# A fused attention and gated MLP kernel: k3 loaded and crossed over ahead of q2 and v2, a gate moved, two bursts regrouped

## The chip, the cores and the metric

The kernel runs on one core of a Trainium2 chip. The metric is the device time of one execution in microseconds (us). Before the change the median of three runs is 245.85 us (245.5 to 246.13).

## The reference

Eight batches of eight heads, 576 tokens and 64 dimensions per head. A packed query p of 32 rows per head first attends to k and v, then q attends to what comes out; the result, as 4608 rows of 512, goes through an MLP whose gate is h * cos(h):

```python
def sm_attn(qq, kk, vv):
    s = scale * np.matmul(qq, kk.transpose(0, 1, 3, 2))
    a = np.exp(s - np.max(s, axis=-1, keepdims=True))
    a = a / (np.sum(a, axis=-1, keepdims=True) + 1e-09)
    return np.matmul(a, vv)
p_packed = sm_attn(p, k, v)                  # (8, 8, 32, 64)
out = sm_attn(q, p_packed, p_packed)         # (8, 8, 576, 64)
x = out.transpose(0, 2, 1, 3).reshape(4608, 512)
h = x @ w_in                                 # 512 -> 2048
return (h * np.cos(h)) @ w_out               # 2048 -> 512
```

## The kernel before

The work goes batch by batch, b = 0 to 7. For a batch, `s1` (L148) makes the scores of p against k, with their exponential on ACT; `a1_pe` or `a1_xbar` (L169, L164) transposes them, on PE or with a DMA transpose; `pp` (L179) multiplies them with v, and `pp_T` (L194) transposes what comes out. `ppw` (L201) multiplies that with w_in in four groups of 512 columns, so that the second attention and the first MLP product become one product with PPW. `s2` (L227) makes the scores of q, `sums2` and `normalise` (L234, L244) their softmax, a2n. Then `h_mm` (L256) makes h in 16 pieces of 128 columns (fc 0 to 15): four matmuls on PE, a cosine on ACT (L267), a product on DVE (L270). The last product, with w_out, is written as a generator, `out_gen` (L343); each step is one matmul of 512 columns, and at the end of a chunk come a copy from PSUM to `osb` and output DMAs on SP's queue. `fill(n)` (L368) takes n such steps of an earlier batch, to occupy PE between other things.

The order on each engine is written out by hand. A front (the code between two slots) holds the attention of the next batch, with `fill` calls in its gaps. `slot(s, hooks, keep, heavy, last)` (L492) holds the 16 `h_mm` of batch s, spreads the remaining output steps over them by weight, leaves `keep` steps over for the next front, and calls hooks, each behind a given fc. A pair in `heavy` gives extra weight to the outputs at an fc, and how many of them come behind the hook. Slots 3 to 6 have one hook, `tiled` (L513), at fc 7: PPW groups 2 and 3 and pp of the next batch in one place, with one evacuation on ACT and one on DVE; pp uses an unused corner of a PSUM bank of `h_mm` (`spare`). Slot 2 has PPW groups 2 and 3 at fc 6 (`pw2`, L509) and pp(3) at fc 9, copied by ACT.

Batches 0 and 1 have their k and q transposed on PE (`pe_T`, L107). In slot 1, k2 is transposed on PE too (`tk2`, L523, at fc 8 and the last third at fc 10), while q2 and k3 are crossed over: `xbar` (L100) issues a DMA transpose from SP's queue. From then on q and k are always crossed over, and a1 from batch 3 on (`a1_xbar`).

Loads are issued by POOL (`load`, L92), in order. `behind(t)` (L96) makes POOL copy one element of a crossed tensor, so that the loads after it wait until that crossing has landed; below this is called the gate. PSUM has three double banks for most of this (`psa`), two single ones for outputs (`O`). There are two buffers each for loaded k and v, one for loaded q, two for crossed k, one for crossed q, and four for `osb`.

Of the kernel before, what the change touches and what calls it, by code (L numbers as in the profile page):

```python
# [15 lines left out]
def kernel(  # L16
# [46 lines left out]
    V, ACT, G = nc.vector, nc.scalar, nc.gpsimd  # L63
# [16 lines left out]
    bf, xT, a1T, sums1, r1, rs1 = {}, {}, {}, {}, {}, {}  # L80
    a2u, lns, a2n, PPW = {}, {}, {}, {}

    def copy(eng, out, in_):
        if eng is ACT:
            ACT.copy(out=out, in_=in_)  # L85
        else:
            eng.tensor_copy(out=out, in_=in_)  # L87

    def psa(dt=FP32):
        return psum["A"].tile([128, 2, 512 if dt == FP32 else 1024], dt, name="psA", tag="A")  # L90

    def load(n, b):  # L92
        bf[n, b] = bf_pool.tile([TP, H, C * D], BF16, name=n + "bf", tag=n + "bf", bufs=1 if n == "q" else 2)
        G.dma_start(out=bf[n, b], in_=srcs[n][b].rearrange("h (p c) d -> p h (c d)", c=C))

    def behind(t):  # L96

        G.tensor_copy(out=gate, in_=t)  # L98

    def xbar(n, b):  # L100
        t = xT[n, b] = att_pool.tile([128, H * 3, TP], BF16, name=n + "T", tag=n + "T", bufs=2 if n == "k" else 1)
        nc.sync.dma_start_transpose(out=t, in_=bf[n, b].rearrange("p h x -> p (h x)"))

    def one(dt=FP32):
        return psum["H"].tile([128, 512 if dt == FP32 else 1024], dt, name="psH", tag="H")

    def pe_T(n, b, engs=(V, V, V), groups=(0, 1, 2), own=None):  # L107
        if 0 in groups:
            xT[n, b] = att_pool.tile([128, H * 3, TP], BF16, name=n + "T", tag=n + "T", bufs=2 if n == "k" else 1)
        t = xT[n, b]  # L110
        flat = bf[n, b].rearrange("p h x -> p (h x)")
        for i in groups:
            ps = own(BF16) if own else psa(BF16)[:, 0, :]
            for j in range(8):
                o = 8 * i + j
                nc.tensor.transpose(ps[:, j * TP:(j + 1) * TP], flat[:, o * 128:(o + 1) * 128],  # L116
                                    ident[0:TP, 0:TP])
            to = t[:, 8 * i:8 * i + 8].rearrange("p a x -> p (a x)"), ps[:, 0:8 * TP]
            if engs[i] is None:
                return to  # L120
            copy(engs[i], *to)

    def bank(dt=FP32):
        return O.tile([128, 512 if dt == FP32 else 1024], dt, name="ot", tag="ot")

    def pack_p(b0, b1, flat=None):
        ng = 2 * (b1 - b0)
        if flat is None:
            flat = psa(BF16).rearrange("p a x -> p (a x)")
        for g in range(ng):  # L130
            nc.tensor.transpose(flat[:, g * 128:(g + 1) * 128],
                                p_bf[:, 2 * b0 + g].rearrange("p t d -> p (t d)"), ident)
        V.tensor_copy(out=P2[:, b0:b1].rearrange("p b h n -> p (b h n)"), in_=flat[:, 0:ng * 128])
# [45 lines left out]
    def pp(b, eng=V, own=None):  # L179

        ps = own() if own else psa()[:, 0, :]
        for y in range(2):
            for j in range(C):
                c = 2 * (j % 3) + j // 3
                for x in range(4):
                    nc.tensor.matmul(ps[32 * x:32 * x + 32, y * D:(y + 1) * D],  # L186
                                     a1T[b][0:TP, y, j, 32 * x:32 * x + 32],
                                     bf["v", b][:, 2 * x + y, c * D:(c + 1) * D],
                                     start=(j == 0), stop=(j == C - 1))
        t = pp_sb[b % 2].rearrange("p a d -> p (a d)")  # L190
        copy(eng, t[:, 0:2 * D], ps[:, 0:2 * D])
        copy(eng, t[:, 2 * D:3 * D], ps[:, 0:D])

    def pp_T(b, eng=V, own=None):  # L194
        ps = own(BF16) if own else psa(BF16)[:, 0, :]
        t = pp_sb[b % 2].rearrange("p a d -> p (a d)")
        for i in range(2):
            nc.tensor.transpose(ps[:, i * 128:(i + 1) * 128], t[:, i * D:i * D + 128], ident)
        copy(eng, ppT[b % 2].rearrange("p i x n -> p (i x n)"), ps[:, 0:256])
# [34 lines left out]
    def sums2(b, y):  # L234
        if b not in lns:
            lns[b] = att_pool.tile([128, 2, S], FP32, name="lns", tag="lns")
        ps = psa()
        for e in range(2):
            nc.tensor.matmul(ps[:, e, 0:HS], ones_blk, a2u[b][:, y, e * HS:(e + 1) * HS],  # L239
                             start=True, stop=True)  # L240
        ACT.activation(out=lns[b][:, y].rearrange("p (e x) -> p e x", e=2),  # L241
                       in_=ps[:, :, 0:HS], func=AF.Ln)
# [55 lines left out]
    def h_rest(b):  # L298

        t = psa()  # L300
        for fc in range(NFC):
            for y in range(2):
                nc.tensor.matmul(t[:, fc // 8, (fc % 8) * 64:(fc % 8) * 64 + 64],  # L303
                                 PPW[b][:, y, fc * 128:(fc + 1) * 128], a2n[b][:, y, 512:576],
                                 start=(y == 0), stop=(y == 1))
        cs = cos_pool.tile([128, 2, 512], BF16, name="cosR", bufs=1)
        ACT.activation(out=cs, in_=t, func=AF.Sin, bias=PI_HALF)
        j0 = (b % 2) * 64
        V.tensor_tensor(out=joint[b // 2][:, :, j0:j0 + 64],
                        in0=t.rearrange("p a (f x) -> p (a f) x", x=64),  # L310
                        in1=cs.rearrange("p a (f x) -> p (a f) x", x=64), op=ALU.mult)
# [53 lines left out]
    def to_do():  # L365
        return sum(n for _, n in filler)

    def fill(n):  # L368
        while n > 0 and filler:
            next(filler[0][0])  # L370
            filler[0][1] -= 1
            if filler[0][1] == 0:
                filler.pop(0)
            n -= 1
# [9 lines left out]
    def dup_p(a, b, eng):  # L384
        for t in range(2):
            eng.tensor_copy(out=p_bf[:, a:b, t, :], in_=p_raw[:, a:b, :])

    def warm(n, wps=None, w=None):
        wps, w = bank() if wps is None else wps, wz if w is None else w
        for _ in range(n):  # L390
            nc.tensor.matmul(wps, w[:, 0:128], w, start=True, stop=True)  # L391
# [45 lines left out]
    pack_p(1, 2, bank(BF16))  # L437
    warm(1)
    sums2(0, 0)
    pe_T("k", 1, (V, V, V), (0,), own=bank)  # L440
    sums2(0, 1)
    pe_T("k", 1, (V, V, V), (1,), own=bank)
    pe_T("k", 1, (V, V, V), (2,), own=bank)
    warm(1)
    normalise(0)
    s1(1)
# [23 lines left out]
    pe_T("q", 1, (ACT, V, V), (1, 2), own=one)  # L470
    rest15()
    warm(3, one())
    load("v", 2)
    load("q", 2)
    load("k", 3)
    dup_p(4, 2 * B, G)
    banks(3)
    set_filler(0)
    s2(1)
    ppw(1, 0, V)  # L480
    fill(2)
    sums2(1, 0)
    fill(1)
    sums2(1, 1)
# [7 lines left out]
    def slot(s, hooks, keep=0, heavy={}, last=None):  # L492


        left = to_do() - keep
        weight = [1 + heavy.get(fc, (0, 0))[0] for fc in range(NFC)]
        for fc in range(NFC):
            rest = h_mm(s, fc)
            if fc == NFC - 1 and last:
                last()  # L500
            rest()
            quota = (left * sum(weight[:fc + 1])) // sum(weight) - (left + keep - to_do())
            behind = min(quota, heavy[fc][1]) if fc in heavy else quota
            fill(quota - behind)
            while hooks and hooks[0][0] == fc:
                hooks.pop(0)[1]()
            fill(behind)

    def pw2(b, n, eng=None):  # L509
        ppw(b, n, eng)  # L510
        ppw(b, n + 1, eng)

    def tiled(b):  # L513


        own, later = spare[0], []
        for n in (2, 3):
            later += ppw(b, n, (ACT, V)[n - 2], later=True)
        later[0]()
        pp(b + 1, V, own=lambda: own)  # L520
        later[1]()
# [10 lines left out]
    def cross(n, b):  # L532
        return lambda: xbar(n, b)

    osb_eng[0] = ACT
    slot(1, [(2, lambda: pw2(1, 2, (ACT, V))), (4, lambda: h_rest(0)), (6, lambda: pack_p(2, 4)), (8, tk2),
             (9, cross("q", 2)), (10, lambda: pe_T("k", 2, (V, V, ACT), (2,))), (12, cross("k", 3))], 4, {2: (1, 2), 4: (3, 5)})
    ACT.preload_act_table_set(EXP_SET)
    osb_eng[0] = V
    behind(xT["k", 3][0:1, 0, 0:1])  # L540
    load("v", 3)
    load("q", 3)
    load("k", 4)
# [33 lines left out]
        load(n, b)  # L577
    fill(9)
    osb_eng[0] = ACT
    slot(2, [(6, lambda: pw2(2, 2)), (9, lambda: pp(3, ACT))], 10, {6: (3, 3), 9: (1, 1)}, lambda: pp_T(3, V))  # L580

    for s in range(3, B):
        nxt = s + 1 < B
# [67 lines left out]
```

## Time and profile before

| | us |
|---|---|
| median of three runs | 245.85 |
| profiled execution, in all | 246.25 |
| its span | 244.5 |
| PE busy in the span | 231.6 |
| ACT, DVE, POOL busy | 166.8, 162.2, 38.1 |
| s2(1) to the first h matmul of slot 1 | 35.63 to 40.60 |
| slot 1: first to last h matmul | 40.60 to 61.25 |
| first gate, second gate (POOL) | 67.16, 89.59 |
| slot 2, first h matmul | 75.09 |
| slot 3, first h matmul | 100.61 |

PE is TensorE's matmuls, PEld its weight loads, DVE VectorE, ACT ScalarE, POOL GpSimd, SP the sync engine; SPq and POOLq are their DMA queues. L12 is line 12 of the kernel. In a line of the timeline come the start, the duration, the engine, the line, the operation, output and inputs, and the count; in brackets stands how long the engine was idle before it and what ended that. A busy time counts overlapping instructions once. In a line of the DMA view the last number is the time from issue to landing. In a line of a table by stretch come the stretch, its length, and for each engine its busy time with the number of instructions; then the granted clock of PE as a share of full speed, the DMA share and GB/s.

### The profile page before, as it was taken

How to read it: one execution, taken by the hardware profiler on the slowest of the kernel's cores; microseconds unless marked ns; L12 is line 12 of the kernel's file. 1: busy time of each engine (PE TensorE's matmuls, PEld its weight loads, DVE VectorE, ACT ScalarE, POOL GpSimd, SP SyncE). 2: the span in 40 equal slices, each digit the busy share in tenths (PEclk: the TensorE clock that was granted, in tenths of full speed). 3: DMA queues.
4: the chain of work that ended last, by engine and by line, in shares of the span. 5: the costliest groups of instructions: out<-in, count | busy, mean ns of one | idle time of the engine just before them, and what ended most of it. 6: DMA issues, size and time to landing. Idle time of an engine off the chain costs nothing.

```text
span 244.5 us, 5460 instructions
## 1 busy us (share of the span) xinstructions
PE 231.6 (95%) x2220; PEld 128.6 (53%) x2255; DVE 162.2 (66%) x257; ACT 166.8 (68%) x269; POOL 38.1 (16%) x61
## 2 busy tenths in 40 slices
PE   7979899999999999999999999999999999999994
PEld 3444254566446464556456554656455645665453
DVE  3349987776568876678758775878657878774001
ACT  2349999778568787877787687858797676774110
POOL 8532330210130023000500510030101010011000
PEclk9999999999999999999999999999999999999999
DMA  6999999999789999999999899989192111312133
GB/s 90 202 211 206 204 208 227 194 232 169 161 137 168 209 174 169 218 185 201 154 214 217 160 213 223 201 163 186 53 198 50 39 46 43 84 29 61 44 86 86
DMA packets 64152, 37.37 MB, mean 153 GB/s; under 512 B 36624, under 2 KB 59536, under 8 KB 64128
## 3 DMA queue, kind: packets, MB, share of 16 engines
q0 software_dynamic: 23184, 18.81, 50.8%
q1 hardware_dynamic: 40704, 18.09, 36.1%
q8 instruction: 17, 0.28, 0.4%
q10 hardware_dynamic: 240, 0.13, 0.2%
q14 instruction: 7, 0.06, 0.1%
HBM read 37.22 MB, written 9.44 MB: 191 GB/s over the span
## 4 chain that ended last, share of the span: by engine, by line
PE 76%; DVE 6%; DMA 5%; issue 2%; ACT 1%; ACTq 0%
PE ot L351 45%; PE psA L263 21%; DMA a1T<-a 5%; DVE gT L295 3%; PE psA L213 3%; PE psA L143 2%; PE ot L337 1%; PE psA L239 1%; DVE PPW L87 1%; PE psA L186 1%; ACT cosT L294 0%; PE psA L116 0%; DVE qT L87 0%; PE psA L303 0%; DVE a1T L87 0%
## 5 line engine op out<-in xcount | busy, mean ns | idle before, releaser
L351 PE MATMUL ot<-w_out_bf,gT 128*128 128x512 bf16 x485 | 128.9, 379 | 1.8 <-issue 1.3
L270 DVE TENSOR_TENSOR gT<-psA,cosT 128x576 bf16<-128x576 f32 x112 | 83.4, 757 | 22.3 <-ACT cosT L267 21.2
L267 ACT ACTIVATE cosT<-psA 128x576 bf16<-128x576 f32 x112 | 73.0, 653 | 24.8 <-PE psA L263 23.5
L263 PE MATMUL psA<-a2n,PPW 128*128 128x288 bf16 x448 | 73.4, 286 | 0.6 <-issue 0.2
L351 PEld LDWEIGHTS <-gT 128*128 128x128 bf16 x512 | 48.2, 98 | 39.7 <-issue 4.6
L263 PEld LDWEIGHTS <-PPW 128*128 128x128 bf16 x448 | 43.7, 98 | 30.5 <-DVE PPW L87 0.5
L87 DVE CAST PPW<-psA 128x1024 bf16<-128x1024 f32 (+1 forms) x24 | 26.8, 1131 | 6.8 <-PE psA L213 6.6
L85 ACT COPY osb<-ot 128x512 f32<-128x512 f32 (+1 forms) x23 | 13.1, 569 | 16.4 <-PE ot L351 14.1
L87 DVE COPY osb<-ot 128x512 f32<-128x512 f32 (+2 forms) x15 | 9.7, 645 | 20.4 <-PE ot L337 17.2
L274 POOL COPY joint<-gT 128x512 bf16<-128x512 bf16 x14 | 8.5, 618 | 76.7 <-DVE gT L270 76.7
L249 DVE SCALAR_TENSOR_TENSOR a2n<-a2u,r,lns 128x576 bf16<-128x576 bf16 x16 | 12.4, 814 | 9.2 <-ACT lns L247 9.2
L241 ACT ACTIVATE lns<-psA 128x576 f32<-128x576 f32 x16 | 10.4, 651 | 8.2 <-PE psA L239 7.7
L152 ACT ACTIVATE a<-psA 128x576 bf16<-128x576 f32 x16 | 10.3, 647 | 8.3 <-PE psA L143 8.2
L98 POOL COPY gate<-kT 1x1 bf16<-1x1 bf16 x5 | 0.9, 180 | 77.3 <-DMA kT<-kbf 77.3
L351 PE MATMUL ot<-w_out_bf,joint 128*128 128x512 bf16 x45 | 11.5, 379 | 0.3 <-issue 0.2
L231 ACT ACTIVATE a2u<-psA,rs 128x576 bf16<-128x576 f32 x16 | 11.0, 737 | 1.1 <-PE psA L143 1.0
L247 ACT ACTIVATE lns<-lns 128x576 f32<-128x576 f32 x16 | 10.0, 673 | 0.0
L213 PE MATMUL psA<-w_in_bf,ppT 64*32 64x512 bf16 x224 | 9.8, 379 | 0.1
L391 PE MATMUL ot<-wz 128*128 128x512 bf16 (+1 forms) x15 | 7.9, 633 | 2.0 <-DVE wz L405 1.7
L295 DVE TENSOR_TENSOR gT<-psH,cosT 128x512 bf16<-128x512 f32 x15 | 9.3, 680 | 0.4 <-ACT cosT L294 0.4
L294 ACT ACTIVATE cosT<-psH 128x512 bf16<-128x512 f32 x15 | 8.4, 625 | 0.7 <-DVE gT L295 0.4
L289 PE MATMUL psH<-a2n,PPW 128*128 128x512 bf16 x28 | 7.3, 381 | 1.0 <-DVE PPW L87 0.8
(91 smaller groups left out, 171.6 us busy)
## 6 DMA issues: line engine op xcount, KB each, us to landing
kbf<-in_k_dram POOLq DMA_DIRECT2D x8, 576.0 KB, 14.3
vbf<-in_v_dram POOLq DMA_DIRECT2D x8, 576.0 KB, 8.5
qbf<-in_q_dram POOLq DMA_DIRECT2D x8, 576.0 KB, 11.0
out_dram<-osb SPq DMA_DIRECT2D x24, 192.0 KB, 2.7
out_dram<-osb SPq DMA_DIRECT2D x22, 128.0 KB, 2.4
w_in_bf<-in_moe_w_in_dram POOLq DMA_DIRECT2D x4, 512.0 KB, 16.3
w_out_bf<-in_moe_w_out_dram POOLq DMA_DIRECT2D x4, 512.0 KB, 20.9
out_dram<-osb SPq DMA_DIRECT2D x25, 64.0 KB, 2.1
```

The source lines that it names most:

```text
L85: ACT.copy(out=out, in_=in_)
L87: eng.tensor_copy(out=out, in_=in_)
L152: ACT.activation(out=a1[b % 2][:, y, :, 0:TP].rearrange("p (e m) x -> p e m x", e=2), in_=ps[y][:, :, 0:HS].rearrange("p e (m x) -> p e m ...
L213: nc.tensor.matmul(ps[y][32 * x:32 * x + 32, :], ppT[b % 2][r, 0, x, :], w_in_bf[r, x, n * 512:(n + 1) * 512], start=True, stop=True)
L231: ACT.activation(out=a2u[b][:, y].rearrange("p (e x) -> p e x", e=2), in_=ps[y][:, :, 0:HS], func=AF.Exp, scale=rs1[b][:, y:y + 1])
L241: ACT.activation(out=lns[b][:, y].rearrange("p (e x) -> p e x", e=2), in_=ps[:, :, 0:HS], func=AF.Ln)
L249: V.scalar_tensor_tensor(out=a2n[b][:, y], in0=a2u[b][:, y], scalar=r1[b][:, y:y + 1], in1=lns[b][:, y], op0=ALU.mult, op1=ALU.mult)
L263: nc.tensor.matmul(ps[:, e, 0:HS], PPW[b][:, y, fc * 128:(fc + 1) * 128], a2n[b][:, y, e * HS:(e + 1) * HS], start=(y == 0), stop=(y == 1))
L267: ACT.activation(out=csv, in_=ps[:, :, 0:HS], func=AF.Sin, bias=PI_HALF)
L270: V.tensor_tensor(out=gT[b][:, fc, :].rearrange("p (e x) -> p e x", e=2), in0=ps[:, :, 0:HS], in1=csv, op=ALU.mult)
L295: return lambda: V.tensor_tensor(out=gT[b][:, fc, 0:512], in0=ps, in1=cs, op=ALU.mult)
L351: nc.tensor.matmul(pss[c], w, w_out_bf[:, fc, :], start=(fc == 0), stop=(fc == NFC - 1))
```

## The change

Five edits. At the start, both `sums2` of batch 0 come ahead of the transposes of k1, which stay together. The three loads v2, q2, k3 are issued in the order k3, q2, v2. In the front ahead of slot 1, `fill(2)` becomes `fill(4)`. In slot 1, k3's crossing moves from fc 12 to fc 7, ahead of q2's (fc 9), and the gate waits for q2's crossing, not k3's. In slot 2, `tiled(2)` at fc 7 replaces `pw2` at fc 6 and `pp(3)` at fc 9.

```diff
     sums2(0, 0)
-    pe_T("k", 1, (V, V, V), (0,), own=bank)
     sums2(0, 1)
-    pe_T("k", 1, (V, V, V), (1,), own=bank)
-    pe_T("k", 1, (V, V, V), (2,), own=bank)
+    pe_T("k", 1, (V, V, V), own=bank)
...
+    load("k", 3)
+    load("q", 2)
     load("v", 2)
-    load("q", 2)
-    load("k", 3)
     dup_p(4, 2 * B, G)
...
     ppw(1, 0, V)
-    fill(2)
+    fill(4)
     sums2(1, 0)
...
     slot(1, [(2, lambda: pw2(1, 2, (ACT, V))), (4, lambda: h_rest(0)), (6, lambda: pack_p(2, 4)),
-             (8, tk2), (9, cross("q", 2)), (10, lambda: pe_T("k", 2, (V, V, ACT), (2,))), (12, cross("k", 3))],
+             (7, cross("k", 3)), (8, tk2), (9, cross("q", 2)), (10, lambda: pe_T("k", 2, (V, V, ACT), (2,)))],
             4, {2: (1, 2), 4: (3, 5)})
...
-    behind(xT["k", 3][0:1, 0, 0:1])
+    behind(xT["q", 2][0:1, 0, 0:1])
     load("v", 3)
     load("q", 3)
     load("k", 4)
...
-    slot(2, [(6, lambda: pw2(2, 2)), (9, lambda: pp(3, ACT))], 10, {6: (3, 3), 9: (1, 1)}, lambda: pp_T(3, V))
+    slot(2, [(7, lambda: tiled(2))], 10, {7: (5, 4)}, lambda: pp_T(3, V))
```

From slot 3 to the end, PE's list of instructions is the same in both kernels.

More of the change, by code (lines that the diff above doesn't have):

```diff
@@ L535 @@
     osb_eng[0] = ACT
-    slot(1, [(2, lambda: pw2(1, 2, (ACT, V))), (4, lambda: h_rest(0)), (6, lambda: pack_p(2, 4)), (8, tk2),
-             (9, cross("q", 2)), (10, lambda: pe_T("k", 2, (V, V, ACT), (2,))), (12, cross("k", 3))], 4, {2: (1, 2), 4: (3, 5)})
+    slot(1, [(2, lambda: pw2(1, 2, (ACT, V))), (4, lambda: h_rest(0)), (6, lambda: pack_p(2, 4)), (7, cross("k", 3)),
+             (8, tk2), (9, cross("q", 2)), (10, lambda: pe_T("k", 2, (V, V, ACT), (2,)))], 4, {2: (1, 2), 4: (3, 5)})
     ACT.preload_act_table_set(EXP_SET)
     osb_eng[0] = V
-    behind(xT["k", 3][0:1, 0, 0:1])
+    behind(xT["q", 2][0:1, 0, 0:1])
     load("v", 3)
```

## The prediction

> **What bounds the kernel now.** I read the busy times first, then the chain that ended last, then PE's busy time slot by slot, and last the queues of SP and POOL around the change.
>
> ```profile
> PE 231.6 (95%) x2220; PEld 128.6 (53%) x2255; DVE 162.2 (66%) x257; ACT 166.8 (68%) x269; POOL 38.1 (16%) x61
> ...
> PE 76%; DVE 6%; DMA 5%; issue 2%; ACT 1%; ACTq 0%
> ```
>
> The chain runs through PE. What can be won is PE's idle time, 244.5 - 231.6 = 12.9 us, and most of that lies outside the change: in the windows 0-36 us and from 232 us on, PE is idle 5.9 and 3.6 us. Next, PE in the five stretches from the first h matmul of slots 2, 3, 4, 5 and 6 to the transposes of pp that end the slot:
>
> ```profile
> core 0: us, PE busy (x) PEld busy (x) DVE busy (x) ACT busy (x) POOL busy (x), PEclk, DMA share, GB/s
> 75.09:90.70 15.61, 15.19 (x156) 9.39 (x157) 12.25 (x18) 12.35 (x21) 0.27 (x2) 1.00 1.24 180
> 100.61:117.13 16.52, 16.12 (x162) 10.10 (x163) 12.93 (x20) 12.08 (x20) 1.49 (x3) 1.00 1.19 195
> 126.97:143.67 16.70, 16.54 (x163) 10.25 (x165) 12.36 (x19) 12.36 (x21) 3.11 (x5) 1.00 1.08 192
> 153.48:170.18 16.70, 16.44 (x163) 10.25 (x165) 12.96 (x20) 11.98 (x20) 2.33 (x4) 1.00 1.05 189
> 179.99:196.70 16.71, 16.55 (x164) 10.26 (x166) 12.36 (x19) 12.37 (x21) 0.62 (x1) 1.00 0.32 72
> ```
>
> The second number is the stretch, the third PE's busy time. Slots 4 to 6, which have the merged burst (both late PPW groups and pp in one place), leave PE idle 0.16, 0.26 and 0.16 us, mean 0.19. Slot 2, which has the burst in two pieces, leaves 0.42. Slot 3 has the merged burst and yet leaves 0.40. The clock is granted in full everywhere.
>
> From PE's timeline, front 1 and slot 3's burst:
>
> ```profile
> 36.22 0.39 PE L351 MATMUL ot<-w_out_bf,gT 128*128 128x512 bf16 x1
> 37.11 0.41 PE L239 MATMUL psA<-a2u,ones_blk 128*128 128x288 bf16 x2 [0.51 <-ACT a2u L231]
> ...
> 109.11 0.55 PE L186 MATMUL psA<-vbf,a1T 96*32 96x64 bf16 x48 [0.19 <-DMA a1T<-a]
> ```
>
> In front 1, PE has run out of output matmuls (one of the two records is missing) and waits for the exponentials of s2(1). At 109.11, pp(4) waits for the crossing (the DMA transpose) of a1 of batch 4. Last, the DMA issues with their time to landing, each from a window at its issue: q2 and k3 at 35, and the crossing of a1 of batch 3 at 69.78:
>
> ```profile
> qbf<-in_q_dram POOLq DMA_DIRECT2D x1, 576.0 KB, 20.6
> kbf<-in_k_dram POOLq DMA_DIRECT2D x1, 576.0 KB, 22.8
> ...
> a1T<-a SPq DMA_TRANSPOSE x1, 14.4
> ```
>
> **Sums of batch 0 ahead of k1.** PE waits at 17.64 for k1's load; sums2(0,1) stands behind the first eight transposes of k1 and moves to about 16.95. Its logarithm on ACT comes at 17.4 instead of 18.44, so the two exponentials of normalise end near 19.2 instead of 20.24. But a2n on DVE (19.82) is queued behind the three copies of kT (18.19 to 19.90), and these wait for k1's load, which nobody moves. DVE then runs without a gap until 24. I take 0. The bounds: 0.2 us lost if the second and third copies came later, 0.15 won because ACT reaches the exponential of s1(1) sooner (20.29, while its matmuls begin at 19.70).
>
> **Two outputs sooner in front 1.** An output matmul costs 2.33 us / 10 = 0.217 us of PE (ten in a row, the last 0.38 long), not the 379 ns shown for one. Two records from 36.22 on fill PE until 36.65; sums2(1,0) starts at 37.11; two more end at 37.09. They fit into 0.46 us of waiting and leave slot 1, whose list has one output less ahead of h_rest and one less ahead of fc 11. Their inputs are there: step 9 of the outputs needs the second quarter of w_out, which lands 17.88 + 20.8 = 38.7; it comes at 38.44 + 3 x 0.217 = 39.1. Slot 1 must be PE-bound for the gain: PE is busy 21.16 of 21.50 us in 41-62.5. The tight places are pack_p (50.83, behind a DVE product that ends at 50.77, itself released by h_rest, which moves along) and fc 11, whose bank is free at 56.43 against 56.70. I take 0.40 of the 0.43; the lower bound is 0.
>
> **k3 ahead of q2 and v2, gate behind q2.** POOL issues k3 where v2 was (30.35), q2 unchanged (35.06), v2 where k3 was (35.83). They land in that order at the old times: 51.75, 35.06 + 20.6 = 55.66 and 35.83 + 22.8 = 58.63. v2 loses 6.9 us; pp(2) needs it only at 67.51. On SP, k3's crossing stands behind the four output DMAs that end at 51.47, and goes at 51.8; it holds SP for 4.36 us, so q2's goes at 56.2, 0.5 us later than now. The two output DMAs of 59.80 move to 60.3; four osb buffers cover that.
>
> When is q2 across? The nearest rows are 122.75 to 133.68: a crossing is issued at 122.75 beside two running loads, the next at 126.88, 0.1 after its load landed, and that one takes 6.8 us, so 10.93 us for the same two crossings beside two loads. From 51.8 that gives 62.7. POOL also has to copy joint ahead of the gate (62.79 + 0.62, less 0.4). So the gate opens near 63.2 instead of 67.16. The bounds: 61.6 (5.4 from 56.2) and 66 (q2's load pushed back to 58.3, then 7.7 as for q3's crossing). k4's load now takes over the buffer of k3 and waits for k3's crossing, which is done before the gate.
>
> [...] If each crossing took the 5.2 us that k4's needs alone (84.23) out of the time of the loads, which need 58.6 - 51.8 = 6.9, both crossings would be done at 51.8 + 6.9 + 10.4 = 69.1, behind today's gate. The trace shows less: q2's crossing ran beside k3's load in 55.73-58.63, the load landed 2.97 us behind the one before it (v2's successor q2, with no crossing beside it, took 3.91), and the crossing still took only 5.4.
>
> **What the earlier gate brings.** The loads v3, q3, k4 follow the gate; k4 lands 84.12 - 67.16 = 16.96 later at most (15.6 in the next but one group). The crossing of a1 is issued at 69.78, when s1(3) is done, which PE's order sets. It landed at 84.18, 109.06 and 131.65, that is 0.05 to 0.8 us behind the k load of its group. With the gate at 63.2, k4 lands by 80.2 and a1T(3) by 80.6. Then k4 crosses some 4 us sooner, the next gate opens near 86 instead of 89.6, k5 lands near 105 (18 us after 86.8), and a1T(4) lands near 105.3 instead of 109.06.
>
> **Merged burst in slot 2.** pp(3) moves from fc 9 to fc 7. In slot 3 it lies 8.50 us behind the slot's start, with 0.2 of waiting; slot 2 has three outputs fewer ahead of it (14 against 17), so 8.50 - 0.2 - 0.65 = 7.65, from 74.7: about 82.35. a1T(3) is there at 80.6. The work is the same 16 + 48 matmuls and four copies, except that pp's two small copies move from ACT (0.38 us) to DVE (0.42). With only ten outputs ahead of fc 7, DVE's product of fc 6 may release the second PPW group up to 0.15 late. Slot 2 should then lose 0.19 idle, as slots 4 to 6, instead of 0.42: a gain of 0.23, bounds 0 and 0.26. In slot 3, a1T(4) no longer holds pp(4), though PE comes 0.63 sooner (109.11 - 0.2 - 0.63 = 108.3 against 105.3): 0.40 - 0.19 = 0.21, bounds 0 and 0.24. From slot 3 on PE's list is the same, matmul for matmul, up to the tail.
>
> **Sum.** 0 + 0.40 + 0.23 + 0.21 = 0.84 us. The profiled execution has 244.5 us in its span and 246.25 in all; it lies 0.4 above the median of the three runs, 245.85 (245.5 to 246.13). The differences should hold for any execution: 245.85 - 0.84 = 245.0.
>
> **Rivals.**
>
> *Half pays*: either the two outputs leave a hole in slot 1 where PE then waits for DVE, or the burst costs DVE what the split cost PE. For it speaks that ACT and DVE have margins of 0.1 to 0.3 us at fc 11 and at the second PPW group; against it, slots 4 to 6 run the same burst with 0.19 idle. 245.85 - 0.40 or - 0.44: 245.4.
>
> *Nothing pays*: the change opens the first gate sooner but not the second (k4's crossing or P's is delayed by the outputs). Then a1T(4) still lands at 109.06 and PE, 0.63 early, waits until 109.1 again. 245.8. Against it: SP has nothing to issue between q3's and k4's crossings.
>
> *Slower*: the crossings of k3 and q2, beside two loads, end no sooner than today. Then a1T(3) still lands at 84.18 and pp(3), now at 82.35, holds PE for 1.85 us. It begins where a1T(3) lands behind 82.35, so with a gate later than 82.35 - 0.4 - 16.96 = 65.0. At a gate of 67.16 the time is 245.85 - 0.40 + 1.85 - 0.2 (slot 3's wait, covered by the delay) = 247.1.
>
> **How the numbers follow.** Forecast 0.58 (245.0, between 244.5 and 245.4 with the bounds of its terms), half pays 0.20, nothing pays 0.10, slower 0.12 (between 246.0 and 247.1). The range 244.5 to 246.1 leaves out most of the slower case and some of the forecast's lower edge; the three runs before spread by 0.6 us, so its ends can't be nearer. A measurement of this kernel can tell about 0.3%, 0.74 us, from no change: 245.11 is the border. Some seven tenths of the forecast lie below it, and a little of half pays: 0.41 + 0.05, faster 0.46. Slower by 0.3% (above 246.6) is most of the slower case and stray causes: 0.12. The rest, 0.42, is within.
>
> **What would show it.** sums2(1,0) without idle time before it; slot 1 0.4 us shorter; the gate near 63 and the next near 86; pp(3) and pp(4) with no wait for a1T; PE idle of about 0.2 in slots 2 and 3. It is wrong if the gate opens after 65, if pp(3) waits, or if PE gets new idle time at fc 11 or at the second PPW group of slot 2.

## The result, and the profile after

The changed kernel takes 245.36 us (median of 22 runs, 244.93 to 245.78), the kernel before, run beside it, 245.78 us (22 runs). The ratio is 0.9982, with a 95% interval of 0.9975 to 0.9990: 0.44 us faster, between 0.25 and 0.61. The profiled execution takes 245.78 us, its span is 244.0.

Of the page of the changed kernel, the busy times and the shares of the chain:

```profile
PE 231.8 (95%) x2220; PEld 129.0 (53%) x2255; DVE 162.5 (67%) x259; ACT 166.0 (68%) x267; POOL 38.1 (16%) x61
...
PE 81%; DVE 6%; issue 2%; ACT 1%; ACTq 0%
```

PE's busy time is the same, the DMA has gone from the chain. PE's timeline of the changed kernel at the places of the three terms (start, duration, engine, line, operation, count; idle before in brackets):

```profile
36.55 1.04 PE L351 MATMUL ot<-w_out_bf,gT 128*128 128x512 bf16 x3
37.45 0.41 PE L239 MATMUL psA<-a2u,ones_blk 128*128 128x288 bf16 x2
...
82.84 0.55 PE L186 MATMUL psA<-vbf,a1T 96*32 96x64 bf16 x48 [0.18 <-DVE gT L270]
...
108.61 0.56 PE L186 MATMUL psA<-vbf,a1T 96*32 96x64 bf16 x48
```

The two more outputs fill the hole ahead of sums2(1,0): no idle time is left before it (one of the four records is missing). pp(3) does not wait for a1T, but 0.18 us for DVE. pp(4) waits for nothing. On SP and POOL:

```profile
51.51 6.82 SPq L102 DMA_TRANSPOSE kT<-kbf  x1
58.45 3.78 SPq L102 DMA_TRANSPOSE qT<-qbf  x1
```

```profile
65.21 0.18 POOL L98 COPY gate<-qT 1x1 bf16<-1x1 bf16 x1 [1.90 <-DMA qT<-qbf]
...
88.24 0.18 POOL L98 COPY gate<-kT 1x1 bf16<-1x1 bf16 x1 [20.51 <-DMA kT<-kbf]
```

k3's crossing goes at 51.5 as forecast, but holds SP for 6.82 us; q2's follows 2.3 us later than forecast, and the gate opens at 65.2, not 63.2.

The two executions can't be laid over each other from zero: in the changed one, k1's load landed 0.34 us later (17.90 against 17.56), with nothing changed ahead of it. So I compare stage lengths, from marks in PE's timeline. All eight experiments are in the table (us):

| kernel | first transpose of k1 | from there to s2(1) | first h of slot 1 to s1(2) | slot 2, first h to pp_T(3) | slot 3, first h to pp(4) |
|---|---|---|---|---|---|
| before | 17.64 | 17.99 | 22.09 | 15.56 | 8.50 |
| changed | 17.97 | 18.00 | 21.66 | 15.42 | 8.24 |
| e1: sums only | 17.09 | 18.20 | 22.01 | 15.55 | 8.24 |
| e2: all but sums | 17.73 | 17.99 | 21.67 | 15.41 | 8.25 |
| e3: fill(4) only | 17.19 | 18.09 | 21.57 | 15.56 | 8.24 |
| e4: burst only | 16.71 | 18.45 | 22.00 | 16.44 | 8.24 |
| e5: gate only | 16.87 | 18.42 | 22.01 | 15.56 | 8.24 |
| e6: without burst | 17.86 | 17.98 | 21.67 | 15.56 | 8.24 |
| e7: old order | 17.77 | 18.00 | 21.66 | 15.42 | 8.24 |
| e8: later burst | 17.16 | 18.16 | 21.46 | 15.38 | 8.23 |

From s2(1) to the first h of slot 1 it is 4.96 or 4.97 in all but e8 (5.13); with it, e8's slot 1 comes to 26.59 against 26.63 in the changed kernel. The profile of the change thus shows 0.43 + 0.14 + 0.26 = 0.83 us of gain behind k1's landing, nearly the forecast 0.84; the times show 0.44. Where is the other half?

### The profile page after: what moved, and what is told of

Same layout as the page of the kernel before. It is cut to its first block, busy times and chain, and to the rows that moved or that the text cites. A ratio compares the mean times of both kernels' runs of the same rounds, so it can differ in the third digit from the quotient of the medians.

```text
span 244.0 us, 5461 instructions
## 1 busy us (share of the span) xinstructions
PE 231.8 (95%) x2220; PEld 129.0 (53%) x2255; DVE 162.5 (67%) x259; ACT 166.0 (68%) x267; POOL 38.1 (16%) x61
## 3 DMA queue, kind: packets, MB, share of 16 engines
q1 hardware_dynamic: 40704, 18.09, 35.7%
## 4 chain that ended last, share of the span: by engine, by line
PE 81%; DVE 6%; issue 2%; ACT 1%; ACTq 0%
PE ot L351 48%; PE psA L263 22%; DVE gT L295 3%; PE psA L213 3%; PE psA L143 2%; PE psA L239 2%; PE ot L337 1%; PE psA L186 1%; DVE gT L270 1%; DVE PPW L87 1%; ACT cosT L267 1%; ACT cosT L294 0%; PE psA L116 0%; DVE qT L87 0%; PE psA L303 0%
## 5 line engine op out<-in xcount | busy, mean ns | idle before, releaser
L270 DVE TENSOR_TENSOR gT<-psA,cosT 128x576 bf16<-128x576 f32 x112 | 83.3, 757 | 21.0 <-ACT cosT L267 19.9
L152 ACT ACTIVATE a<-psA 128x576 bf16<-128x576 f32 x16 | 10.2, 646 | 9.5 <-PE psA L143 9.5
## 6 DMA issues: line engine op xcount, KB each, us to landing
qbf<-in_q_dram POOLq DMA_DIRECT2D x8, 576.0 KB, 10.2
```

Source lines behind the costliest of these rows:

```text
L152: ACT.activation(out=a1[b % 2][:, y, :, 0:TP].rearrange("p (e m) x -> p e m x", e=2), in_=ps[y][:, :, 0:HS].rearrange("p e (m x) -> p e m ...
L270: V.tensor_tensor(out=gT[b][:, fc, :].rearrange("p (e x) -> p e x", e=2), in0=ps[:, :, 0:HS], in1=csv, op=ALU.mult)
```

## The experiments

**Two theories.** A: the first edit costs what is missing. sums2(0,1) waits for ACT and now stands ahead of k1's transposes, which costs time whenever k1 lands early. B: the first edit is worth nothing, and the 0.26 us of slot 3 are missing from a usual execution of before.

**e1, the first edit alone.**

```diff
     sums2(0, 0)
-    pe_T("k", 1, (V, V, V), (0,), own=bank)
     sums2(0, 1)
-    pe_T("k", 1, (V, V, V), (1,), own=bank)
-    pe_T("k", 1, (V, V, V), (2,), own=bank)
+    pe_T("k", 1, (V, V, V), own=bank)
```

> The kernel before with the first edit alone (both sums of batch 0 ahead of k1's transposes). Theory A (the edit costs time: sums2(0,1), which waits for the exponentials of s2(0), now stands ahead of the transposes of k1, and delays them whenever k1 lands before about 17.2 us): 0.2 to 0.4 us slower than before, and all kernels with this edit lose as much. Theory B (the edit is worth nothing, as forecast, and the change gained only half because a term of the later slots is smaller in a usual execution than in the one profiled): within 0.1 us of before.

Measured: ratio 1.0005 (0.9995 to 1.0015), that is between 0.12 us faster and 0.37 slower; the times alone don't tell A from B. Nor does the table, as it stands: the first transpose of k1 is itself moved by the edit. So I go back to what sets it, the landing of k1's load and the start of sums2(0,0).

k1 landed at 17.56 to 17.90 us in before, the changed kernel, e2 and e7. There PE waits for the load, and s2(1) follows the first transpose by 17.99 or 18.00 us, with the edit (the changed kernel) and without (the other three). The edit costs nothing.

k1 landed at 16.13 to 16.41 in the other six. There the first transpose starts 0.24 us after sums2(0,0) without the edit (e3, e4, e5), and 0.87 to 0.88 after it with the edit (e1, e6, e8). The delay of which A speaks is there. In e1 and e8 it hardly shows: sums2(0,0) starts early, at 16.22 and 16.29, and s2(1) comes at 35.29 and 35.32, against 35.16 to 35.29 in the three without the edit. In e4 and e5, PE waits 0.17 and 0.16 us for q1's load ahead of q1's transposes, so being earlier wins nothing there. In e6 sums2(0,0) starts late, as in e3, and the delay remains. PE's timeline of e3, without the edit:

```profile
16.95 0.41 PE L239 MATMUL psA<-a2u,ones_blk 128*128 128x288 bf16 x2 [0.31 <-ACT a2u L231]
17.19 0.51 PE L116 MATMUL ot<-ident,kbf 96*128 96x96 bf16 x8
17.58 0.41 PE L239 MATMUL psA<-a2u,ones_blk 128*128 128x288 bf16 x2
...
35.28 0.44 PE L143 MATMUL psA<-qT,ppT 64*32 64x288 bf16 x16 [0.22 <-DVE qT L87]
```

and of e6, with it:

```profile
16.98 0.41 PE L239 MATMUL psA<-a2u,ones_blk 128*128 128x288 bf16 x2
17.61 0.41 PE L239 MATMUL psA<-a2u,ones_blk 128*128 128x288 bf16 x2 [0.23 <-ACT a2u L231]
17.86 0.84 PE L116 MATMUL ot<-ident,kbf 96*128 96x96 bf16 x16
...
35.84 0.44 PE L143 MATMUL psA<-qT,ppT 64*32 64x288 bf16 x16 [0.22 <-DVE qT L87]
```

s2(1) comes 0.56 us later in e6, of which 0.03 was there at sums2(0,0). Most of it is there at s1(1), 19.78 against 19.28, ahead of everything else in which the two kernels differ. So the edit costs nothing in some executions and about 0.5 us in others; A is right for the latter. How often they come, no run shows; none of the 11 runs of e1 is below 245.62 us, and 16 of the 35 runs of before beside it are.

**e2, the change without the first edit** (the diff is against the changed kernel).

```diff
     sums2(0, 0)
+    pe_T("k", 1, (V, V, V), (0,), own=bank)
     sums2(0, 1)
-    pe_T("k", 1, (V, V, V), own=bank)
+    pe_T("k", 1, (V, V, V), (1,), own=bank)
+    pe_T("k", 1, (V, V, V), (2,), own=bank)
```

> The changed kernel without the first edit. Theory A: about 245.0, that is 0.6 to 0.85 us below before and 0.2 to 0.4 below the changed kernel. Theory B: 0.42 us below before, as the changed kernel.

Measured: 0.9989 (0.9976 to 1.0002), 0.27 us faster, and no better than the changed kernel. That speaks against a loss of the size that A had in mind, 0.6 to 0.85 us below before, though the interval is wide. Its profile can't help: k1 landed late in it, at 17.68.

**e3, two outputs sooner, alone.**

```diff
-    fill(2)
+    fill(4)
     sums2(1, 0)
```

> The kernel before with fill(4) for fill(2) alone. In the profile of the changed kernel slot 1 is 0.43 us shorter. If pp(4) in slot 3 has no slack to the crossing of a1 (its landing is set by the second gate, which does not move here), PE comes 0.43 us sooner and waits for a1T: slot 3's wait grows from 0.2 to about 0.6 and the time stays within 0.1 us of before. If a1T of batch 4 usually lands earlier than in the execution that was profiled, the 0.4 us remain.

Measured: 0.9991 (0.9977 to 1.0006), between 0.56 us faster and 0.15 slower; from s2(1) to s1(2) 26.54 us, against 27.06 before and 26.97 to 26.98 in e1, e4 and e5. So 0.43 us are won against those three, and slot 3 does not take them back: it reaches pp(4) after 8.24 us, with the old gate. The crossings of a1 of batch 4, in the DMA view, from windows at their issue, with the time to landing; e1 (issued 96.14), e3 (95.73) and e4 (96.89):

```profile
a1T<-a SPq DMA_TRANSPOSE x1, 11.2
```

```profile
a1T<-a SPq DMA_TRANSPOSE x1, 11.0
```

```profile
a1T<-a SPq DMA_TRANSPOSE x1, 10.6
```

They land at 107.3, 106.7 and 107.5, and pp(4) starts at 108.43, 108.02 and 109.18: 1.1 to 1.7 us to spare. In the profile of before it landed at 109.06, when pp(4) had been due for 0.2 us. None of the three has the wait that the forecast counted. PE was not earlier in before: e4's slot 3 starts at 100.94, before's at 100.61. The loads were slower: k5's, ahead of the crossing, took 16.5 us in before and 14.8, 14.5 and 14.9 in e1, e3 and e4. The times hint that such executions are rare: the profiled one of before took 246.25 us, and of the 86 runs of before that were timed beside the others, 10 took longer; one with the wait and an early k1 would not show in that count. B stands for slot 3; its other half, that the first edit is worth nothing, does not hold in every execution (e1).

**e4, the merged burst alone**, with the old gate, as the slower rival has it.

```diff
-    slot(2, [(6, lambda: pw2(2, 2)), (9, lambda: pp(3, ACT))], 10, {6: (3, 3), 9: (1, 1)}, lambda: pp_T(3, V))
+    slot(2, [(7, lambda: tiled(2))], 10, {7: (5, 4)}, lambda: pp_T(3, V))
```

> The kernel before with the merged burst of slot 2 alone, so with the old gate. The forecast's slower rival: a1T of batch 3 lands near 84.2, pp(3) is due at about 82.8 (82.84 with the start of the profile of the changed kernel, slot 2 from 74.99), so PE waits 1.3 to 1.5 us there, keeps some 0.2 for slot 3's wait, and the time is 1.0 to 1.4 us above before. If the crossing of a1 is not held by the loads behind the gate, pp(3) does not wait and the time falls by 0.1 to 0.2.

Measured: 1.0035 (1.0008 to 1.0063), 0.86 us slower. PE's timeline of e4:

```profile
81.56 0.63 PE L213 MATMUL psA<-w_in_bf,ppT 64*32 64x512 bf16 x16
83.40 0.56 PE L186 MATMUL psA<-vbf,a1T 96*32 96x64 bf16 x48 [1.21 <-DMA a1T<-a]
```

a1T lands at 83.3 (69.22 + 14.1), pp(3) is due at 82.2. The wait of 1.21 us makes slot 2 0.88 longer than before (16.44 against 15.56). The rival was real; only the earlier gate keeps the change from it.

**e5, loads, crossing and gate alone.**

```diff
+    load("k", 3)
+    load("q", 2)
     load("v", 2)
-    load("q", 2)
-    load("k", 3)
...
-             (9, cross("q", 2)), (10, lambda: pe_T("k", 2, (V, V, ACT), (2,))), (12, cross("k", 3))], 4, {2: (1, 2), 4: (3, 5)})
+             (7, cross("k", 3)), (8, tk2), (9, cross("q", 2)), (10, lambda: pe_T("k", 2, (V, V, ACT), (2,)))], 4, {2: (1, 2), 4: (3, 5)})
...
-    behind(xT["k", 3][0:1, 0, 0:1])
+    behind(xT["q", 2][0:1, 0, 0:1])
```

> The kernel before with the loads, the crossing of k3 and the gate as in the change, and nothing else. Theory B (the wait of pp(4) for a1T in the profile of before belongs to that execution; e1, e3 and e4, with the old gate, do not have it): the first gate opens near 65, a1T of batch 3 lands near 81.5 and nobody waits for it; the time is that of before, within 0.1 us. Rival (in a usual execution PE does wait for a1T of batch 4, and the profiles of e1, e3 and e4 are the lucky ones): 0.2 us below before.

Measured: 0.9996 (0.9979 to 1.0014). a1T of batch 3 lands at 81.6, pp(3) in its old place starts at 84.92, no stage is shorter. As B has it: the earlier gate wins nothing by itself. The interval is too wide to exclude the rival's 0.2 us, and this profile can't exclude it either, since it has the new gate. Against the rival stand e1, e3 and e4, three profiles with the old gate and no wait, and the times named there.

**e6, the change without the burst** (against the changed kernel).

```diff
-    slot(2, [(7, lambda: tiled(2))], 10, {7: (5, 4)}, lambda: pp_T(3, V))
+    slot(2, [(6, lambda: pw2(2, 2)), (9, lambda: pp(3, ACT))], 10, {6: (3, 3), 9: (1, 1)}, lambda: pp_T(3, V))
```

> The changed kernel with slot 2 as before. Theory B: slot 1 keeps its 0.43 us, slot 2 takes 15.56 again and not 15.42, slot 3 reaches pp(4) after 8.24: 0.4 below before. Rival (the two outputs are worth less on average than in the profiles, and the burst more): within 0.2 of before.

Measured: 0.9989 (0.9977 to 1.0002), between 0.56 us faster and 0.05 slower, so the times don't decide; slots 1, 2 and 3 take 21.67, 15.56 and 8.24, as theory B says. Ahead of them, this profile is the one in which the first edit cost about 0.5 us.

**e7, the gate behind q2, in the old order of loads and crossings.**

```diff
-    behind(xT["k", 3][0:1, 0, 0:1])
+    behind(xT["q", 2][0:1, 0, 0:1])
```

and fill(4) and the merged burst.

> The gate behind q2, the merged burst and fill(4), but the loads and the crossings in the old order (v2, q2, k3; k3 crosses at fc 12, so about 62, when the gate opens). It asks whether k3 has to go first. If a crossing beside three fresh loads lands with the last of them, as a1T(3) does: k3 lands between 68 and 78, s1(3), due at 67.5, waits for it up to 10 us, and the time is 1 to 10 us above before. If it takes 7 to 10 us, as crossings beside two loads did: k3 lands at 69 to 72, PE waits 1.5 to 4.5 us. If the order does not matter: 0.4 to 0.6 below before, as the changed kernel.

Measured: 1.0191 (1.0149 to 1.0233), 4.7 us slower. k3's crossing, issued at 60.71, landed 10.2 us later, at 70.9. PE's timeline of e7, and three stretches (length, busy times, and, third from the end, PE's granted clock):

```profile
67.22 0.55 PE L186 MATMUL psA<-vbf,a1T 96*32 96x64 bf16 x48
70.93 0.68 PE L143 MATMUL psA<-kT,P 64*32 64x288 bf16 x16 [3.16 <-DMA kT<-kbf]
```

```profile
60.00:67.00 7.00, 7.00 (x59) 3.52 (x56) 4.15 (x8) 3.96 (x7) 2.97 (x5) 1.00 1.01 154
...
70.90:74.40 3.50, 3.47 (x24) 1.11 (x24) 0.53 (x3) 1.37 (x4) 0.00 (x0) 0.50 1.24 252
74.40:77.00 2.60, 2.60 (x31) 0.95 (x30) 1.23 (x1) 1.37 (x2) 0.00 (x0) 0.56 1.32 207
```

s1(3) waits 3.2 us for k3, as the second answer in the expectation had it. Then comes what nobody expected: the granted clock is 0.50 in the 3.5 us after it and 0.56 on average in the next 2.6. The stages from pp(2) to s2(2) and from there to slot 2 are 4.84 and 1.04 us longer than in the changed kernel, 5.88 together, of which the wait itself is 3.2. So k3 has to go first; the gate alone can't be moved.

**e8, more outputs ahead of the burst** (against the changed kernel).

```diff
-    slot(2, [(7, lambda: tiled(2))], 10, {7: (5, 4)}, lambda: pp_T(3, V))
+    slot(2, [(7, lambda: tiled(2))], 10, {7: (6, 3)}, lambda: pp_T(3, V))
```

> The changed kernel with {7: (6, 3)} in slot 2: seven outputs, not four, ahead of the burst. Theory: in the profile of the changed kernel pp(3) waits 0.18 us for DVE's product of fc 7, whose bank pp shares; with three outputs more ahead of it DVE is done, and slot 2 takes 15.25 us and not 15.42: 0.15 to 0.2 below the changed kernel, 0.6 below before. Rival (the outputs are missing behind the burst, where PE then waits for the copies of pp and PPW on DVE): slot 2 at 15.4 or more.

Measured: 0.9980 (0.9965 to 0.9996), which can't be told from the changed kernel. PE's timeline of e8:

```profile
81.78 0.62 PE L213 MATMUL psA<-w_in_bf,ppT 64*32 64x512 bf16 x16
82.33 0.55 PE L186 MATMUL psA<-vbf,a1T 96*32 96x64 bf16 x48
...
88.63 0.38 PE L351 MATMUL ot<-w_out_bf,joint 128*128 128x512 bf16 x1
89.03 0.65 PE L263 MATMUL psA<-a2n,PPW 128*128 128x288 bf16 x4
```

The wait ahead of pp(3) is gone, but slot 2 takes 15.38 us, not 15.25: the outputs are missing later, and h matmul 15 comes 0.18 us behind the one output ahead of it (88.63 + 0.217 = 88.85). That is the rival: the hole has moved. No version that clearly beats the changed kernel came out of this.

## Why the prediction was right and wrong

The time, 245.36, lies in the range (244.5 to 246.1), and the kernel is faster, as forecast. The gain is half of the 0.84 us forecast: 0.18%, inside the border of 0.3%, where the forecast had it just beyond.

- *Sums of batch 0, 0 us*: right for the execution that the forecast read, in which PE waits for k1 until 17.64, and for the profile of the changed kernel. Not right for every execution: where k1 has landed before sums2(0,0), its transposes start 0.63 us later behind sums2(0,1). That cost about 0.5 us in e6, beyond the bound of 0.2.
- *Two outputs sooner, 0.40*: right. 0.43 (27.06 to 26.63 from s2(1) to s1(2)), the whole price of two matmuls (2 x 0.217): slot 1 is PE-bound, with PE busy for 21.32 of its 21.66 us (40.94 to 62.60).
- *The gate at 63.2*: the mechanism was right, the place 2 us off. The step that failed is "it holds SP for 4.36 us", taken from a crossing with no load beside it. Beside two loads k3's crossing held SP for 6.82 us and landed after 9.7. The bound of 66 held. The estimate that was weighed against the change, in which each crossing takes its 5.2 us out of the time of the loads, gave 69.1, the row used gave 62.7; 65.2 lies between. The two loads behind k3's landed 8.2 us after it (59.46 against 51.25), in before the two behind v2's 6.9: with the crossings among them the loads lost some 1.3 us, not 10.4. Two of the forecast's signs of being wrong came true, a gate after 65 and a wait of pp(3), and the next gate opened at 88.24, not near 86. It was enough: a1T(3) landed at 81.8 (69.68 + 12.1), 0.9 us ahead of 82.66, when pp(3) was due.
- *Merged burst, 0.23*: mis-sized, 0.14. The text named DVE's late product of fc 6 as a risk and then took the idle time of slots 4 to 6, which have six outputs ahead of the burst where slot 2 has four. The wait came, 0.18 us, at pp(3), for the product of fc 7, whose bank pp shares. e8 shows that moving outputs does not win it back.
- *Slot 3, 0.40 - 0.19 = 0.21*: this is the term that failed; it is 0 in the other profiles with the old gate. It rested on one wait in one execution, behind loads that were 1.6 to 2.0 us slower than in the others. With the old gate, e1, e3 and e4 reach pp(4) in 8.24 us, as the changed kernel does.

With these sizes the sum is 0.43 + 0.14 + 0 = 0.57 us, and less in the executions in which the first edit costs time; the measured 0.44 (0.25 to 0.61) agrees. Of the rivals, half pays (245.4) came nearest in size, though for another reason than either it gave. The slower case was placed rightly: with the gate left where it was, e4 is 0.86 us slower. It was priced too high, since a1T(3) there landed 1.1 us, not 1.85, behind pp(3).

What stays open: how often the first edit costs its 0.5 us, and how often the kernel before waits for a1T of batch 4. The intervals of the parts, 0.5 to 1.4 us wide in e1 to e6 and e8, are wider than the terms, so the split between them rests on stage lengths in single profiles. From slot 2 on, these agree within 0.02 us where a stage has the same code and no DMA in its way.

## What to carry to other kernels

A wait for a DMA in one profile may be that execution's alone: set the stage beside the same stage in other executions before it enters a sum. A stage length is worth nothing if the edit moves its starting mark: the first transpose of k1 hid the cost of the first edit until its two causes were read. A hole on the bounding engine is worth what can be moved into it, provided that the stage it is taken from is bound by that engine too. When a consumer is moved forward, as pp(3) here, look for what sets its input's landing and move that first: the order edit earned nothing, and without it the burst would have cost 0.86 us.

## What the runs showed of the hardware

- k3's crossing took longer to land beside loads, and held its queue longer: beside two loads in the changed kernel it took 9.7 us to land and 6.82 of SP, with none beside it in the profile of before 6.2 and 4.36; k4's, with none either, 5.2 and 3.74 there. q2's in before, beside k3's load until 58.63, took 5.4 and 4.02. a1T of batch 3, beside three loads, took 12.1 to 14.4 us to land in before, the changed kernel, e4, e5, e6 and e8, but only 4.1 to 5.1 of SP in the five of them other than e4. It landed 0.06 us behind the last of the loads in before and 0.5 in the changed kernel; k3's landed 1.7 behind.
- In e7 PE had no work for 3.2 us, from 67.77 on. Its granted clock was 1.00 from 60.0 to 67.0, 0.87 on average from 67.0 to 70.9, 0.50 from 70.9 to 74.4, 0.56 from 74.4 to 77.0 and 1.00 from 77.0 to 80.0. If it went from 1.00 to 0.50 and back in one step each, these means put the fall at 69.9, some 2.1 us into the wait, and the return at 76.7, some 5.8 us after work began (an estimate: 3.9 x 0.13 / 0.5 = 1.0 us before 70.9, and 2.6 x 0.44 / 0.5 = 2.3 us after 74.4). In e4, with 1.21 us without work before 83.40, the mean is 1.00 from 82.0 to 84.0 and from 83.4 to 88.0. With what followed, the stall of 3.2 us in e7 cost 5.9.
- k1's load, with the same code ahead of it, landed at 16.13 to 16.41 us in six of the ten profiles and at 17.56 to 17.90 in four. s2(1) followed at 35.16 to 35.32 in five of the six (35.84 in e6) and at 35.63 to 35.97 in the four. This start alone spreads the times by up to 0.8 us, as much as the change was forecast to win.
